# Loading and converting w1 and w2 three to four slots earlier in a fused attention and MoE kernel

## The chip, the cores and the metric

The kernel runs on one core of a Trainium2 chip. The metric is the time of one execution on the device in microseconds. Five engines have instruction queues of their own and each works its queue in order: PE (TensorE, matrix products and transposes), DVE (VectorE), ACT (ScalarE), POOL (GpSimd) and SP (SyncE, which here issues every DMA).

## What is computed

Attention over pooled keys and values, then a gated two-layer product over all tokens:

```python
# q, k, v: (8 batches, 8 heads, 576 tokens, 64)
k_p = k.reshape(B, H, 72, 8, D).mean(axis=3)
v_p = v.reshape(B, H, 72, 8, D).mean(axis=3)
scores = scale * q @ k_p^T
attn = softmax(scores)              # over 72 pooled keys
x = (attn @ v_p) as (4608 tokens, 512)
a = x @ w1                          # w1, w2: (512, 1024)
b = x @ w2
out = (a * b @ w3) @ w_out          # w3: (1024, 1024), w_out: (1024, 512)
```

The kernel multiplies w3 and w_out once, to `W = w3 @ w_out` (1024 x 512), and then has only `out = (a * b) @ W` to do for each token.

## The kernel before

The tokens are worked in 12 chunks of 384. Every fp32 operand is split into a high part and a remainder, and each product is made of three matrix products (high x high, high x low, low x high; `PASSES`).

There are three stages. In W (slots 4 to 36 of the plan, up to about 86.8 us) PE builds `W` from 16 steps `w_mm(s)`. Steps 0 to 7 are W's first half, steps 8 to 15 its second half. In the second half the attention of chunk 0 is worked as well. From slot M0 = 36 on the main loop runs: for each chunk m and each of eight column blocks j, `a_mm` and `b_mm` (L563), the gate (L573, L583, L584, L589) and `out_mm` (L598), with the attention of the next chunk in between.

Nothing is scheduled by a tool. Each piece of work is entered by `at(kind, slot, function, ...)`, with a kind of L (loads), P (post-processing on DVE, ACT and POOL), M (main matmuls) or A (attention matmuls). The whole plan is sorted by the integer part of the slot, then by kind in the order L, P, M, A, then by the fraction. So a slot sets the order in which each engine's instructions are written, and never a time. An engine that has to wait in its queue holds up everything behind it.

What the change and the prediction touch:

- The weights arrive as 512 KB cells (`load_w12`, the DMA at L126), 16 of them for w1 and w2, j = 0 to 7 and w = 0 or 1; cell i = 2j + w. They are written into buffers that the W stage has used (`FREED`): even cells into the place of a block of w_out, free when PE has made `w_mm(8 + j)`; odd cells into places of w3.
- `w12_conv` takes the two 32-bit halves of each number in a cell: ACT makes the high part `z` (L135), DVE shifts the other (L140). `w12_conv2` joins them on DVE (L148). `w12_split` makes the two parts for the matmul: a cast on ACT (L152) and a difference (L153), on POOL or, for three cells (`LO_DVE`), on DVE. The buffers of the conversion are called `wb`, of the w3 cells `Wc`, of the loaded cells `raw` and of the finished parts `hl`.
- The same helper lines work for w3 (`Wc<-raw`, then `hl<-att` after a turn on PE), and L153 and L152 also split W's accumulators at the end of W (`Wc<-b`, `Wc<-o`).
- The softmax of one tile of a chunk: `s_mm` (PE, L404), `mx` (DVE, L420), then either L422 (DVE) and an exponential on ACT (L425) and L426 (DVE), or four exponentials on ACT with their sums (L430; the tiles in `SOFT_ACT`); then L439, L441, L442 (DVE). R is a small remainder of it (L451 on ACT, L453 on DVE). PE turns E and R (L464, L474), ACT and DVE split the result (L520, L521, L527).
- All attention work on PE shares three PSUM tiles named `att`, so L474 of one tile waits until the scores of the next tile have been read.
- `load_q3` (L286) loads q for chunks 0 and 1, PE turns it (L295), ACT copies it (L301). `load_vr` (L356) loads the first and last pooled rows of v, which end up in `VR`. `load_k` (L307) and `prep_k` (L319 on DVE, L362 to L364 on POOL) pool k, and PE turns the result (L328). `av_mm` is L537 to L540, its split L548 and L549.

Of the kernel before, what the change touches and what calls it, by code (L numbers as in the profile page):

```python
# [18 lines left out]
def kernel(  # L19
# [617 lines left out]
    def at(kind, k, fn, *args):  # L637


        plan.append((k // 1, "LPMA".index(kind), k % 1, len(plan), fn, args))  # L640
# [53 lines left out]
    K0 = F0 + 2 * NJ  # L694
    M0 = F0 + 2 * NS
# [6 lines left out]
    for s in range(NS):  # L702
        k = F0 + 2 * s
# [19 lines left out]
    for j in range(NJ):  # L723
        for w in range(2):
            i = 2 * j + w
            at("L", K0 + 8.5 + i, load_w12, j, w)
            k = M0 - 6 + 1.25 * i
            at("P", k, w12_conv, j, w)
            at("P", k + 1, w12_conv2, j, w)
            at("P", k + 4, w12_split, j, w)  # L730


    for m in range(NCH):
        m0 = M0 + 3 * NJ * m
        for j in range(NJ):
            k = m0 + 3 * j
# [9 lines left out]
    for n in range(1, NCH):  # L746
        k = M0 + 3 * NJ * (n - 1)
# [8 lines left out]
    for b in range(1, B):  # L756
        k = M0 + 3 * NJ * (3 * (b // 2) + b % 2 - 1)
# [39 lines left out]
```

## Time and profile before

| | us |
|---|---|
| median of three runs | 786.11 |
| lowest and highest run | 785.08, 788.28 |
| the profiled execution | 787.77 |
| its span, first to last instruction | 785.9 |
| PE busy | 759.7 (97%) |
| DVE busy | 479.2 (61%) |
| ACT busy | 278.5 (35%) |
| POOL busy | 201.1 (26%) |

The mean granted clock of PE is 0.991 of full speed. Of the chain of work that ended last, PE has 74% of the span and DVE 15%.

How to read the rows: a group's row has its line in the kernel, the engine, the operation, the tile written and the tiles read (buffer numbers left out), shapes, and "x" with the number of instructions; then busy us and the mean in ns of one; then the idle time of the engine ahead of them and what ended it. A row of the timeline has the start in us from the span's start, the duration in us, and the same names; the idle time ahead of it stands in brackets with what ended it. A row of the waits reads: engine, tile and line that waited, what it waited for, us in total, times, longest. The rows themselves stand in the prediction.

### The profile page before, as it was taken

The page shows a single profiled execution, that of the slowest core. Times are in us where ns is not written, and L with a number is a line of the kernel's source. Part 1 is how long each engine was busy: PE and PEld are TensorE (multiplying, and loading weights), DVE is VectorE, ACT ScalarE, POOL GpSimd, SP SyncE. Part 2 cuts the span into 40 slices and gives each one's busy share as a digit, 9 for nine tenths or more (in the row PEclk, how much of TensorE's full clock was granted, in tenths as well). Part 3 has the DMA queues.
Part 4 walks back from the last instruction along what each step waited for, and adds up shares of the span by engine and source line. Part 5 has one row for each costly group of instructions (what it writes and reads, how often), then busy time and mean ns, then how long its engine had stood idle before and what let it go on. Part 6 is the DMA issues. An engine that isn't in the chain of part 4 may idle for free.

```text
span 785.9 us, 11514 instructions
## 1 busy us (share of the span) xinstructions
PE 759.7 (97%) x4146; PEld 703.7 (90%) x4146; DVE 479.2 (61%) x939; ACT 278.5 (35%) x694; POOL 201.1 (26%) x234
## 2 busy tenths in 40 slices
PE   8898888999999999999999999999999999999998
PEld 7677777899999998999999998999999998999997
DVE  6957988576475477476484586574574675662211
ACT  5566655332233233232233233332332333332211
POOL 2254564204307403005208202016125220000000
PEclk9999999999999999999999999999999999999999
DMA  9998970016326332036144223037144232120101
GB/s 328 292 209 200 282 152 10 1 61 129 66 79 134 71 98 55 16 86 140 32 129 93 77 81 71 15 101 140 41 122 94 75 75 47 47 55 1 40 1 41
DMA packets 123913, 74.43 MB, mean 95 GB/s; under 512 B 75600, under 2 KB 107600, under 8 KB 123856
## 3 DMA queue, kind: packets, MB, share of 16 engines
q1 hardware_dynamic: 123856, 73.69, 38.2%
q8 instruction: 33, 0.54, 0.3%
q14 instruction: 24, 0.20, 0.1%
HBM read 52.43 MB, written 9.44 MB: 79 GB/s over the span
## 4 chain that ended last, share of the span: by engine, by line
PE 74%; DVE 15%; ACT 3%; DMA 3%; issue 3%; SPq 1%; DVEq 0%
PE o L598 22%; PE a L563 21%; PE b L563 21%; PE att L404 3%; DMA st<-in_v_dram 2%; PE o L624 2%; DVE T L487 2%; DVE E L442 1%; DVE wb L148 1%; DVE wb L140 1%; PE att L538 1%; PE att L540 1%; PE att L539 1%; DVE mx L420 1%; PE att L537 1%
## 5 line engine op out<-in xcount | busy, mean ns | idle before, releaser
L563 PE MATMUL a<-xT,hl 128*128 128x384 f32 x1152 | 222.1, 341 | 0.0
L563 PE MATMUL b<-xT,hl 128*128 128x384 f32 x1152 | 220.8, 339 | 0.4 <-DVE Wc L153 0.4
L563 PEld LDWEIGHTS a<-xT,hl 128*128 128x128 f32 x1152 | 202.5, 189 | 4.5 <-POOL hl L153 0.2
L563 PEld LDWEIGHTS b<-xT,hl 128*128 128x128 f32 x1152 | 199.7, 188 | 0.8 <-DVE Wc L153 0.8
L598 PE MATMUL o<-Wc,gh 128*128 128x512 f32 x576 | 180.6, 395 | 0.0
L362 POOL TENSOR_TENSOR st<-st 72x512 f32<-72x512 f32 (+1 forms) x53 | 77.8, 1469 | 224.5 <-DMA st<-in_k_dram 172.1
L598 PEld LDWEIGHTS o<-Wc,gh 128*128 128x128 f32 x576 | 106.7, 188 | 17.0
L583 DVE TENSOR_TENSOR a<-b,a 128x384 f32<-128x384 f32 x96 | 52.8, 550 | 112.6 <-PE b L563 112.6
L598 PE MATMUL o<-Wc,gl 128*128 128x512 f32 x288 | 114.3, 397 | 3.1 <-DVE gl L589 3.1
L584 ACT CAST gh<-a 128x384 fp32r<-128x384 f32 x96 | 49.2, 513 | 154.8 <-DVE a L583 154.8
L573 ACT COPY a<-a 128x384 f32<-128x384 f32 x96 | 46.0, 479 | 109.8 <-PE a L563 88.0
L425 ACT ACTIVATE E<-E 128x288 f32<-128x288 f32 (+1 forms) x70 | 31.1, 445 | 123.4 <-DVE E L422 123.4
L589 DVE TENSOR_TENSOR gl<-a,gh 128x384 fp32r<-128x384 f32 x96 | 64.0, 667 | 13.0 <-ACT gh L584 13.0
L598 PEld LDWEIGHTS o<-Wc,gl 128*128 128x128 f32 x288 | 54.1, 188 | 16.9 <-DVE gl L589 4.4
L549 DVE TENSOR_TENSOR xT<-att,xT 128x384 fp32r<-128x384 f32 x48 | 26.5, 556 | 60.3 <-ACT xT L548 60.3
L375 POOL TENSOR_TENSOR vbd<-vm,vbd 64x256 fp32r<-64x256 f32 x16 | 12.1, 759 | 180.1 <-ACT vbd L374 179.5
L426 DVE TENSOR_REDUCE sm<-E 128x4 f32<-128x288 f32 (+1 forms) x70 | 31.6, 452 | 35.8 <-ACT E L425 35.8
L404 PE MATMUL att<-kbd,qT 128*128 128x144 f32 (+1 forms) x320 | 52.6, 288 | 0.2 <-ACT E L430 0.2
L404 PEld LDWEIGHTS att<-kbd,qT 128*128 128x128 f32 (+1 forms) x320 | 47.8, 180 | 4.3 <-ACT E L430 0.5
L153 DVE TENSOR_TENSOR PTx<-PTx,PTh 128x512 fp32r<-128x512 f32 (+1 forms) x33 | 24.7, 749 | 35.1 <-ACT PTh L152 31.7
L420 DVE TENSOR_REDUCE mx<-att 128x4 f32<-128x288 f32 (+1 forms) x80 | 35.3, 441 | 17.7 <-PE att L404 17.6
L363 POOL TENSOR_TENSOR st<-st 72x256 f32<-72x256 f32 (+1 forms) x53 | 44.4, 837 | 4.2
(91 smaller groups left out, 811.6 us busy)
## 6 DMA issues: line engine op xcount, KB each, us to landing
raw<-in_moe_w_dram SPq DMA_DIRECT2D x32, 512.0 KB
PTx<-T SPq DMA_DIRECT2D x120, 96.0 KB
st<-in_k_dram SPq DMA_DIRECT2D x32, 288.0 KB
out_dram<-ob SPq DMA_DIRECT2D x35, 256.0 KB
st<-in_v_dram SPq DMA_DIRECT2D x32, 256.0 KB
qs<-in_q_dram SPq DMA_DIRECT2D x128, 48.0 KB
raw<-in_moe_w_out_dram SPq DMA_DIRECT2D x8, 512.0 KB
st<-in_v_dram SPq DMA_DIRECT2D x64, 64.0 KB
```

The costliest lines, as they stand in the source:

```text
L362: nc.gpsimd.tensor_tensor(out=t[:, :, 0:4], in0=t[:, :, 0:4], in1=t[:, :, 4:8], op=ALU.add)
L363: nc.gpsimd.tensor_tensor(out=t[:, :, 0:2], in0=t[:, :, 0:2], in1=t[:, :, 2:4], op=ALU.add)
L404: nc.tensor.matmul(out=ps[:nt, 2 * KP * j:2 * KP * (j + 1)], lhsT=qT[n][:, pr, off:off + nt], rhs=kbd[b % 2][:, pr], start=True, stop=True,)
L420: nc.vector.tensor_reduce(out=mx[:nt, hs], in_=sv, axis=AX.X, op=ALU.min)
L425: nc.scalar.activation(out=E[:nt, hs], in_=E[:nt, hs], func=AF.Exp, scale=-1.0)
L426: nc.vector.reduce_sum(out=sm[:nt, hs], in_=E[:nt, hs], axis=AX.X)
L563: nc.tensor.matmul(out=o, lhsT=w12[j, w][sw][:, kt * P:(kt + 1) * P], rhs=x[sx][:, kt], start=(i == 0), stop=(i == 3 * NK - 1))
L573: nc.scalar.copy(out=a, in_=gt[m, j][:, :CH])
L583: nc.vector.tensor_tensor(out=g, in0=ps[:, :CH], in1=g, op=ALU.mult)
L584: nc.scalar.copy(out=gh, in_=g)
L589: nc.vector.tensor_tensor(out=gl, in0=g, in1=f(gh), op=ALU.subtract)
L598: nc.tensor.matmul(out=oacc[m][t], lhsT=(gh, gl)[sg][:, c], rhs=W[j][sw], start=(j == 0 and i == 0), stop=(j == NJ - 1 and i == 2))
```

## The change

The loads of w1 and w2 (kind L) stand four slots earlier, the conversions (kind P) start three slots earlier, with 1.4 slots from cell to cell instead of 1.25. The last cell's conversion thus moves from slot 48.75 to slot 48. Nothing else is edited, and the number of instructions is the same on every engine.

```diff
     for j in range(NJ):
         for w in range(2):
             i = 2 * j + w
-            at("L", K0 + 8.5 + i, load_w12, j, w)
-            k = M0 - 6 + 1.25 * i
+            at("L", K0 + 4.5 + i, load_w12, j, w)
+            k = M0 - 9 + 1.4 * i
             at("P", k, w12_conv, j, w)
             at("P", k + 1, w12_conv2, j, w)
             at("P", k + 4, w12_split, j, w)
```

What that does to the queues is seen at three places. The first is W's second half, at 63 to 71 us of the profile. On DVE (L140 and L148 on `wb` are conversions of w1 and w2, on `Wc` of w3):

```order
 L140 TENSOR_SCALAR Wc<-raw 128x512
+L140 TENSOR_SCALAR wb<-raw 128x512
 L521 TENSOR_TENSOR PTx<-att,PTh 128x4x4x32
 L420 TENSOR_REDUCE mx<-att 128x4
 L148 SCALAR_TENSOR_TENSOR Wc<-Wc 128x512
 L420 TENSOR_REDUCE mx<-att 128x4
+L148 SCALAR_TENSOR_TENSOR wb<-wb 128x512
+L140 TENSOR_SCALAR wb<-raw 128x512
 L153 TENSOR_TENSOR hl<-att,hl 128x512
 L439 TENSOR_SCALAR sm<-sm 128x8
```

Two L140 and one L148 now stand ahead of the softmax row L439; before, the first of them stood behind it. On SP, which issues the loads, a little earlier (46 to 61 us):

```order
 L120 DMA raw<-in_moe_w_dram 128x4x256 x2
+L126 DMA raw<-in_moe_w_dram 128x4x256
 L356 DMA st<-in_v_dram 32x1x512 x8
-L126 DMA raw<-in_moe_w_dram 128x4x256
+L126 DMA raw<-in_moe_w_dram 128x4x256 x4
 L286 DMA qs<-in_q_dram 64x3x64 x4
 L307 DMA st<-in_k_dram 72x2x512
```

Of the 16 loads (L126) one stands ahead of the v loads now, and five instead of one ahead of the first q loads of chunk 1.

The second place is the passage from W to the main loop, on ACT (86 to 90 us):

```order
 L301 COPY qT<-att 128x3x128 x2
-L135 ACTIVATE wb<-raw 128x512
 L152 CAST Wc<-b 128x512
 L152 CAST Wc<-o_560 128x512
```

A conversion that stood between the copies of q and the casts of W's accumulators stands further ahead now. The third place is tile (1, 1) of the softmax on DVE (111 to 119 us). Before:

```order
L420 TENSOR_REDUCE mx<-att 96x4
L148 SCALAR_TENSOR_TENSOR wb<-wb 128x512
L140 TENSOR_SCALAR wb<-raw 128x512
L583 TENSOR_TENSOR a<-b,a 128x384
L420 TENSOR_REDUCE mx<-att 96x4
L589 TENSOR_TENSOR gl<-a,gh 128x384
L148 SCALAR_TENSOR_TENSOR wb<-wb 128x512
L140 TENSOR_SCALAR wb<-raw 128x512
L439 TENSOR_SCALAR sm<-sm 96x8
```

Now:

```order
L420 TENSOR_REDUCE mx<-att 96x4
L148 SCALAR_TENSOR_TENSOR wb<-wb 128x512
L153 TENSOR_TENSOR hl<-wb,hl 128x512
L140 TENSOR_SCALAR wb<-raw 128x512
L583 TENSOR_TENSOR a<-b,a 128x384
L420 TENSOR_REDUCE mx<-att 96x4
L589 TENSOR_TENSOR gl<-a,gh 128x384
L148 SCALAR_TENSOR_TENSOR wb<-wb 128x512
L439 TENSOR_SCALAR sm<-sm 96x8
```

A split on DVE (L153, cell 9, which is j = 4, w = 1) has come up behind the first `mx`, and one L140 has left.

## The prediction

> **What bounds the kernel now.** I read the page first, then the table of stretches, then PE's waits in the stretch that is not full, then what DVE does there.
>
> ```profile
> span 785.9 us, 11514 instructions
> PE 759.7 (97%) x4146; PEld 703.7 (90%) x4146; DVE 479.2 (61%) x939; ACT 278.5 (35%) x694; POOL 201.1 (26%) x234
> ```
>
> PE is busy 97% of the span, so only 26 us are not PE. The stretches say where these lie (columns: stretch, length, busy us and instructions of PE, PEld, DVE, ACT, POOL, granted clock, DMA share, GB/s):
>
> ```profile
> 86.80:142.20 55.40, 45.53 (x253) 41.28 (x252) 50.20 (x82) 32.87 (x98) 29.47 (x25) 0.97 0.52 117
> 142.20:157.00 14.80, 14.80 (x90) 14.09 (x89) 7.19 (x14) 5.01 (x12) 2.58 (x3) 1.00 0.00 1
> 37.00:86.80 49.80, 46.41 (x237) 38.09 (x238) 37.38 (x66) 32.10 (x102) 28.08 (x28) 0.93 0.93 216
> ```
>
> The first row is the start of the main loop: its first matmul of `a` runs at 86.80, and there PE is idle for 55.40 - 45.53 = 9.87 us, while DVE is busy for 50.20 of 55.40. The second row is what follows: PE has no idle time at all, so a time won before 142.2 goes through to the end and nothing behind it takes it back. The third is W's second half, whose DVE has 12.4 us free. PE's waits in the first stretch, by cause:
>
> ```profile
> PE att L474 <- ACT E L430: 4.8, 2, 3.9
> PE att L474 <- DVE E L422: 2.0, 1, 2.0
> PE att L328 <- DVE km L319: 1.6, 1, 1.6
> ```
>
> Nearly all of it is softmax work for chunk 1 or the pooled k of batch 1, which DVE or ACT delivers late; where ACT is named (L430) it had itself been waiting for DVE's `mx`, the instruction ahead of it. So in this stretch the chain runs along DVE's queue, in which the conversion of w1 and w2 stands between the softmax instructions:
>
> ```profile
> L148 DVE SCALAR_TENSOR_TENSOR wb<-wb 128x512 int32<-128x512 int32 x12 | 12.3, 1023 | 0.9 <-ACT wb L135 0.8
> L140 DVE TENSOR_SCALAR wb<-raw 128x512 int32<-128x512 int32 x11 | 9.3, 849 | 0.0
> ```
>
> That is 21.6 of DVE's 50.2 us. What ends 9.87 us of idle PE is therefore DVE's queue from about 70 us on (before that it waits for others) to about 141.
>
> **The change, term by term.** Nothing is added or removed; 16 loads, and for each cell two DVE conversions, two ACT instructions and a split, change their places. So the sum counts what leaves DVE's chain between 70 and 141 us, and which waits in it go or come.
>
> (a) Work that leaves the chain. By the order of DVE's rows, two L140 and one L148 now stand ahead of the softmax rows of 70.57 us, where DVE waits today:
>
> ```profile
> 67.64 0.46 DVE L420 TENSOR_REDUCE mx<-att 128x4 f32<-128x288 f32 x1 [1.96 <-PE att L404]
> 69.96 0.69 DVE L153 TENSOR_TENSOR hl<-att,hl 128x512 fp32r<-128x512 f32 x1 [1.87 <-ACT hl L152]
> 70.57 0.16 DVE L439 TENSOR_SCALAR sm<-sm 128x8 f32<-128x8 f32 x1
> ...
> 141.38 0.34 DVE L453 TENSOR_TENSOR R<-E,R 96x64 fp32r<-96x64 f32 x2
> ```
>
> The two waits of 1.96 and 1.87 us hide them. From 70.57 to 141.38, where the last softmax tile of chunk 1 is handed to PE, 14 L140 and 15 L148 remain of 16 and 16. Their price is one of two, by whether POOL runs beside them:
>
> ```profile
> 115.69 1.78 DVE L148 SCALAR_TENSOR_TENSOR wb<-wb 128x512 int32<-128x512 int32 x1
> ...
> 120.70 0.68 DVE L148 SCALAR_TENSOR_TENSOR wb<-wb 128x512 int32<-128x512 int32 x1
> ...
> 121.94 0.41 DVE L140 TENSOR_SCALAR wb<-raw 128x512 int32<-128x512 int32 x1
> ```
> ```profile
> 115.31 1.60 POOL L362 TENSOR_TENSOR st<-st 128x512 f32<-128x512 f32 x1
> ...
> 118.14 0.52 POOL L364 TENSOR_TENSOR vm<-st 128x128 f32<-128x128 f32 x1
> 124.51 1.29 POOL L153 TENSOR_TENSOR hl<-wb,hl 128x512 fp32r<-128x512 f32 x1 [5.85 <-ACT hl L152]
> ```
>
> L148 takes 1.78 us beside a POOL instruction and 0.68 where POOL is silent (118.66 to 123.2 or later). At the short price the three are 0.68 + 2 x 0.41 = 1.50 us; at the means of the stretch (1.023 and 0.849) they are 2.72. POOL loses none of its instructions, so what it stretches today it can stretch in the next DVE instruction; I take 1.50, and keep 2.72 for the range. [...]
>
> (b) The wait ahead of W's last split. ACT converts a cell (L135) just ahead of the cast of `Wc` for which DVE waits:
>
> ```profile
> 87.68 0.65 ACT L135 ACTIVATE wb<-raw 128x512 f32<-128x512 f32 x1
> 88.23 0.58 ACT L152 CAST Wc<-b 128x512 fp32r<-128x512 f32 x1
> ```
> ```profile
> 88.84 0.69 DVE L153 TENSOR_TENSOR Wc<-b,Wc 128x512 fp32r<-128x512 f32 x1 [1.00 <-ACT Wc L152]
> ```
>
> In the new order that L135 is gone from there. The cast starts 88.23 - 87.68 = 0.55 us earlier, and DVE's wait of 1.00 shrinks by as much: **-0.55**.
>
> (c) A wait for ACT in the middle:
>
> ```profile
> 123.95 0.69 DVE L148 SCALAR_TENSOR_TENSOR wb<-wb 128x512 int32<-128x512 int32 x1 [0.77 <-ACT wb L135]
> ```
>
> Here L135 stands behind four exponentials on ACT. In the new order the L135 of the cell concerned stands ahead of them: **-0.77**.
>
> (d) A wait that is new. DVE's split of cell (4,1) moves up to right behind `mx` of tile (1,1), and the cast on ACT that it needs stands behind the four exponentials that this very `mx` releases:
>
> ```profile
> 111.61 1.31 ACT E L430 x8
> ```
> ```profile
> 113.38 0.62 ACT L152 CAST hl<-wb 128x512 fp32r<-128x512 f32 x1
> 113.89 0.52 ACT L584 CAST gh<-a 128x384 fp32r<-128x384 f32 x1
> ```
>
> The cast takes 113.89 - 113.38 = 0.51, start to start. So DVE waits 1.31 + 0.51 - 0.68 (the L148 that runs meanwhile) = 1.14 us. Queued behind it are L140, the product L583 and the second `mx`. In exchange the old wait of `gl` there falls from
>
> ```profile
> 114.44 1.33 DVE L589 TENSOR_TENSOR gl<-a,gh 128x384 fp32r<-128x384 f32 x1 [0.87 <-ACT gh L584]
> ```
>
> 0.87 to about 0.1, since L583 is now later than ACT's other work: **+0.4**.
>
> (e) On ACT one L135 now stands ahead of the cast that ends DVE's wait of 1.87 at 69.96; L135 takes 0.55 of ACT's time by the rows of (b) (start to start): **+0.55**, as that cast lies on the chain.
>
> Sum: -1.50 - 0.55 - 0.77 + 0.4 + 0.55 = **-1.87 us**; with the dear price in (a) it is -3.1. PE has 9.87 us of waits, so the gain is not capped by it. The profiled execution took 787.77 us (span 785.9 and 1.9 around it): 785.9 after. It was 1.66 above the median of the runs shown, 786.11; on that scale the forecast is **784.2 us**.
>
> What I cost at nothing: the loads themselves. They are taken from one queue on SP, and the first now waits there for PE to release its cell, with the eight small loads of v (L356) behind it. The cover is between POOL and ACT:
>
> ```profile
> 62.15 1.37 POOL L362 TENSOR_TENSOR st<-st 128x512 f32<-128x512 f32 x1 [6.38 <-DMA st<-in_v_dram]
> ...
> 64.60 0.46 POOL L364 TENSOR_TENSOR vrm<-st 128x128 f32<-128x128 f32 x1
> ```
> ```profile
> 69.80 0.33 ACT L381 CAST vrh<-vrm 128x128 fp32r<-128x128 f32 x1
> ```
>
> POOL has the sum at 65.06 and ACT takes it at 69.80, so 4.7 us late is free. Without this cover each further us would delay `VR`, which PE needs for the first attention product. The loads of q and k that follow are a rival below.
>
> **Rivals.**
>
> The stretch by POOL falls away (779). The cells come one per 1.4 slots instead of 1.25, so POOL's splits and DVE's conversions could overlap less. If the nine L148 and nine L140 that stand behind W's last split drop from their means to the short price, that saves 9 x (1.02 - 0.68) + 9 x (0.85 - 0.41) = 7.0 us; the waits of PE (9.87) allow it: 786.11 - 7.0 = 779.1. For it speaks that DVE ends early in each slot once it is ahead; against it, that POOL has the same instructions in 55 us in which it is busy for 29.47. Chance 0.2.
>
> The q of chunk 1 comes late (790). Four more loads of 512 KB stand ahead of its last pieces than before, and PE turns these directly ahead of its first matmul of `a`:
>
> ```profile
> 75.54 1.18 SPq L286 DMA_DIRECT2D qs<-in_q_dram  x2
> ```
> ```profile
> 81.54 1.80 SPq L126 DMA_DIRECT2D raw<-in_moe_w_dram  x1
> ```
> ```profile
> 86.03 1.02 PE L295 MATMUL att<-ident,qs 128*128 128x128 f32 x6 [0.24 <-DVE xT L549]
> ```
>
> The last q load is issued at 76.1. A load waits for the one eight places ahead in the queue, which puts its landing at 81.5 or earlier. At the 216 GB/s of the stretch, four loads take 4 x 2.4 = 9.7 us. If none of that is hidden, q lands at 91.2, 4.8 us after PE's need at 86.4; ACT's copy of q and the cast of `Wc` behind it wait as long, so the chain starts 4.8 late. Less the 1.87 won this is +2.9, and with the slow matmuls that follow so long an idle time +4.3: 790.4. That price is from the matmuls right behind the wait of 3.9 above, against the same 12 matmuls of `a` a little later, 3.71 - 2.35 = 1.4:
>
> ```profile
> 113.26 3.71 PE L563 MATMUL a<-xT,hl 128*128 128x384 f32 x12
> ...
> 123.58 2.35 PE L563 MATMUL a<-xT,hl 128*128 128x384 f32 x12
> ```
>  Against this: from 52 to 68 us DMA is not full:
>
> ```profile
> 52.00:56.00 4.00, 3.19 (x22) 2.74 (x21) 2.01 (x5) 3.22 (x21) 2.44 (x3) 1.00 0.63 174
> 56.00:60.00 4.00, 4.00 (x22) 3.30 (x21) 2.75 (x8) 2.88 (x16) 0.00 (x0) 1.00 0.68 199
> 60.00:64.00 4.00, 1.71 (x11) 1.03 (x10) 3.97 (x9) 2.31 (x8) 1.77 (x2) 1.00 0.83 183
> 64.00:68.00 4.00, 4.00 (x18) 3.53 (x18) 1.95 (x4) 1.69 (x9) 0.98 (x2) 0.63 0.64 145
> ```
>
> These free shares are 4 x (0.37 + 0.32 + 0.17 + 0.36) = 4.9 us, and that leaves 4.8 of the 9.7: landing at 86.3, just in time. It decides from 86.4 on. Chance 0.14.
>
> Nothing is left (786 to 787). If (d) comes at its full 1.1 us, (a) is hidden by waits of DVE for PE, and only (b) counts, the sum is about 0 to +1. Chance 0.16.
>
> **How the numbers follow.** Forecast (782.5 to 786) 0.5, rivals 0.2, 0.14 and 0.16. About 0.5%, 3.9 us, is what a measurement of this kernel can tell from no change: the runs shown lie 3.2 us apart. Faster by more (below 782.2) takes the first rival and the edge of the forecast with the dear price: 0.28. Slower (above 790.0) takes most of the q rival: 0.13. Within: 0.59. The range leaves out the far end of the first rival and of the second: 778.5 to 789.5.
>
> **What would show it.** (a): two L140 and one L148 before 70 us inside DVE's waits; the stretch from the first `a` to the last softmax tile shorter by 2 to 3 us, with DVE still nearly full. (b), (c): the waits of 1.00 and 0.77 shorter or gone. (d): DVE's L153 on `wb` with a wait of about 1.1 us for ACT. (e): the cast at 69.33 half a us later. The forecast is wrong if PE waits for DMA at L295, if the means of L148 and L140 in the stretch fall to 0.7 and 0.4, or if PE's wait at L474 (3.9) stays as long as it is.

## The result and the profile after

The changed kernel takes 782.41 us (median of 20 runs, 780.73 to 788.11), the kernel before 787.96 us (20 runs, 783.82 to 791.66). The ratio is 0.9935, 95% interval 0.992 to 0.9951. A second comparison (e1 below) gave 0.9942, 0.9924 to 0.996. By the ratios the change wins 4.6 to 5.1 us. The forecast, 784.2 us, named the side, and the time lies inside its whole range (778.5 to 789.5), a little below the part that was held likeliest (782.5 to 786). Of the gain it had only 1.9 us. That the two times lie only 1.8 us apart is partly luck: the forecast starts from 786.11 us (three runs of the kernel before), and its 20 runs have 787.96. From there 1.9 us less is 786.1, and the changed kernel is 3.7 us below that.

The profiled execution of the changed kernel took 788.11 us, the longest of its 20 runs. A second profile (e1) took 784.20 us, the median of its own runs, and is the one meant where only one is shown. First its page:

```profile
span 782.4 us, 11499 instructions
PE 758.8 (97%) x4146; PEld 702.9 (90%) x4146; DVE 477.4 (61%) x939; ACT 279.0 (36%) x694; POOL 201.9 (26%) x234
```

The page alone hides the change: PE is busy 97% in both. The stretches show it. They are cut at events that every profile has: the first turn of R in W's second half (L474), the first matmul of `a` (L563), and the last turn of R of chunk 1. The part between the first two is called the tail of W here, the part between the last two the main stage. Columns as in the prediction: length, busy us and instructions of PE, PEld, DVE, ACT, POOL, granted clock, DMA share, GB/s. The tail and the main stage before:

```profile
63.65:86.80 23.15, 22.86 (x116) 18.99 (x117) 18.96 (x30) 15.20 (x45) 13.72 (x15) 0.93 0.95 226
86.80:141.86 55.06, 45.20 (x250) 40.94 (x249) 49.87 (x81) 32.53 (x98) 29.13 (x25) 0.97 0.53 118
```

The same two and what follows them in the profile of 788.11 us:

```profile
65.78:93.70 27.92, 24.66 (x117) 20.02 (x117) 24.70 (x34) 16.74 (x48) 15.89 (x17) 0.88 1.04 239
93.70:142.17 48.47, 44.31 (x250) 40.99 (x249) 43.52 (x78) 30.94 (x94) 26.86 (x23) 0.96 0.41 97
142.17:157.00 14.83, 14.83 (x93) 14.17 (x91) 7.28 (x13) 4.94 (x11) 3.49 (x4) 1.00 0.00 1
```

And in the second profile:

```profile
63.42:89.75 26.33, 23.06 (x116) 18.74 (x117) 24.44 (x34) 17.06 (x49) 17.58 (x18) 0.94 0.92 251
89.75:138.22 48.47, 44.35 (x250) 40.95 (x249) 43.52 (x78) 30.96 (x94) 26.86 (x23) 0.96 0.45 104
```

Three things are to be seen. The main stage is 6.59 us shorter (55.06 to 48.47), the same in both profiles: DVE works 6.35 us less there, and PE's idle time falls from 9.86 to 4.12. The tail of W is longer, by 3.18 in the second profile and 4.77 in the first: DVE works 5.48 us more in it (18.96 to 24.44), and PE, which had almost no idle time inside it, has 3.27. Behind the last turn of R PE is full as before. From there to the end the three profiles take 645.91, 645.94 and 645.98 us, so nothing is won or lost behind it. Stage by stage in us, with the time ahead of the first turn cut once more at the first product of column block `b` in W:

| | to the first `b` of W | to the first turn of R | tail of W | main stage | to the end | whole |
|---|---|---|---|---|---|---|
| before | 45.77 | 17.88 | 23.15 | 55.06 | 645.91 | 787.77 |
| changed, second profile | 46.61 | 16.81 | 26.33 | 48.47 | 645.98 | 784.20 |
| difference | +0.84 | -1.07 | +3.18 | -6.59 | +0.07 | -3.57 |

The first column is ahead of everything that the change moves, and scatters from execution to execution (44.2 to 48.1 us in all profiles). Without it the change wins 4.4 us by these two profiles. That this is near the 4.6 to 5.1 of the many runs is a matter of which profiles are compared: the profile of 788.11 us, with 18.38 us to the first turn of R and a tail of 27.92, gives 1.3 us against the same one before, and a second profile of the kernel before (e2) gives 7.4 us against the second of the change. So the gain as a whole is read from the many runs, and from single profiles only what repeats: the main stage.

PE's waits in the main stage, second profile:

```profile
PE att L404 <- ACT E L430: 1.7, 1, 1.7
PE att L328 <- DVE km L319: 1.7, 1, 1.7
PE att L474 <- DVE E L422: 0.7, 1, 0.7
```

The long wait at L474 (3.9 of the 4.8 that the prediction quoted) is gone, with the slow matmuls that followed it (twelve in 3.71 us). Other slow ones are there: the twelve behind the wait of 1.7 us at L328 take 3.22 us instead of 2.35. What is left are three waits, and none is for DMA.

### The profile page after: what moved, and what is told of

It reads as the page before. It is cut to its first block, busy times and chain, and to the rows that moved or that the text cites. A ratio compares the mean times of both kernels' runs of the same rounds, so it can differ in the third digit from the quotient of the medians.

```text
span 786.3 us, 11499 instructions
## 1 busy us (share of the span) xinstructions
PE 760.7 (97%) x4146; PEld 704.5 (90%) x4146; DVE 479.3 (61%) x939; ACT 278.7 (35%) x694; POOL 198.1 (25%) x234
## 4 chain that ended last, share of the span: by engine, by line
PE 75%; DVE 14%; ACT 4%; DMA 4%; issue 2%; SPq 0%; DVEq 0%
PE o L598 22%; PE a L563 21%; PE b L563 21%; PE att L404 3%; PE o L624 2%; DVE T L487 2%; DMA st<-in_k_dram 2%; DVE E L422 1%; DVE mx L420 1%; DVE E L442 1%; ACT E L425 1%; PE att L538 1%; DVE wb L140 1%; PE att L540 1%; PE att L539 1%
## 5 line engine op out<-in xcount | busy, mean ns | idle before, releaser
L563 PE MATMUL b<-xT,hl 128*128 128x384 f32 x1152 | 222.0, 341 | 0.0
L563 PE MATMUL a<-xT,hl 128*128 128x384 f32 x1152 | 220.6, 339 | 0.0
L563 PEld LDWEIGHTS a<-xT,hl 128*128 128x128 f32 x1152 | 201.1, 188 | 4.4 <-DVE xT L549 0.2
L563 PEld LDWEIGHTS b<-xT,hl 128*128 128x128 f32 x1152 | 200.7, 189 | 0.2 <-DVE Wc L153 0.2
L362 POOL TENSOR_TENSOR st<-st 72x512 f32<-72x512 f32 (+1 forms) x53 | 73.3, 1383 | 229.9 <-DMA st<-in_k_dram 177.4
L583 DVE TENSOR_TENSOR a<-b,a 128x384 f32<-128x384 f32 x96 | 52.8, 550 | 110.1 <-PE b L563 110.1
L589 DVE TENSOR_TENSOR gl<-a,gh 128x384 fp32r<-128x384 f32 x96 | 63.5, 662 | 13.5 <-ACT gh L584 13.5
L375 POOL TENSOR_TENSOR vbd<-vm,vbd 64x256 fp32r<-64x256 f32 x16 | 12.2, 760 | 177.5 <-ACT vbd L374 177.1
L404 PEld LDWEIGHTS att<-kbd,qT 128*128 128x128 f32 (+1 forms) x320 | 48.1, 181 | 6.0 <-ACT E L430 2.1
L426 DVE TENSOR_REDUCE sm<-E 128x4 f32<-128x288 f32 (+1 forms) x70 | 31.6, 452 | 35.9 <-ACT E L425 35.9
L153 DVE TENSOR_TENSOR PTx<-PTx,PTh 128x512 fp32r<-128x512 f32 (+1 forms) x33 | 26.9, 815 | 35.1 <-ACT PTh L152 32.9
L624 PE MATMUL o<-hl 128*128 128x512 f32 x144 | 44.3, 446 | 3.9 <-DVE hl L177 3.9
L420 DVE TENSOR_REDUCE mx<-att 128x4 f32<-128x288 f32 (+1 forms) x80 | 35.3, 441 | 17.6 <-PE att L404 17.6
```

What stands on the lines that cost most here:

```text
L362: nc.gpsimd.tensor_tensor(out=t[:, :, 0:4], in0=t[:, :, 0:4], in1=t[:, :, 4:8], op=ALU.add)
L404: nc.tensor.matmul(out=ps[:nt, 2 * KP * j:2 * KP * (j + 1)], lhsT=qT[n][:, pr, off:off + nt], rhs=kbd[b % 2][:, pr], start=True, stop=True,)
L420: nc.vector.tensor_reduce(out=mx[:nt, hs], in_=sv, axis=AX.X, op=ALU.min)
L426: nc.vector.reduce_sum(out=sm[:nt, hs], in_=E[:nt, hs], axis=AX.X)
L563: nc.tensor.matmul(out=o, lhsT=w12[j, w][sw][:, kt * P:(kt + 1) * P], rhs=x[sx][:, kt], start=(i == 0), stop=(i == 3 * NK - 1))
L583: nc.vector.tensor_tensor(out=g, in0=ps[:, :CH], in1=g, op=ALU.mult)
```

## Experiments

Every ratio is against the kernel before on the same chip. Tail and main stage are from the one profile of each kernel.

| label | what it is | ratio (95%) | profiled us | tail | main stage |
|---|---|---|---|---|---|
| e1 | the changed kernel again | 0.9942 (0.9924 to 0.996) | 784.20 | 26.33 | 48.47 |
| e2 | the kernel before again | 1.0008 (0.9991 to 1.0025) | 791.35 | 24.15 | 55.53 |
| e3 | loads alone | 1.0000 (0.9987 to 1.0012) | 788.54 | 23.64 | 55.18 |
| e4 | conversions alone | 0.9973 (0.996 to 0.9986) | 786.43 | 25.87 | 48.53 |
| e5 | loads, earlier start, old pace | 0.9991 (0.9973 to 1.0009) | 786.61 | 26.19 | 50.58 |
| e6 | loads, old start, new pace | 1.0016 (0.9999 to 1.0032) | 788.70 | 23.24 | 54.35 |
| e7 | all splits on DVE | 0.999 (0.9973 to 1.0006) | 787.53 | 24.45 | 52.83 |
| e8 | first load behind v's | 0.9974 (0.9955 to 0.9993) | 785.27 | 27.93 | 48.49 |
| e9 | first split a slot later | 0.9923 (0.9892 to 0.9953) | 783.36 | 26.19 | 48.42 |
| e10 | first two splits 1.5 slots later | 0.9956 (0.9937 to 0.9976) | 783.94 | 25.81 | 48.46 |
| e11 | one step further up | 0.9998 (0.9981 to 1.0016) | 789.45 | 26.48 | 52.52 |
| e12 | e9 again | 0.9925 (0.9898 to 0.9951) | 782.18 | 24.38 | 48.44 |

### e1, e2: how far the profiles repeat

No edit: the two kernels again.

> The changed kernel once more, for a second profile, since the profiled execution of it (788.11 us) lies 5.7 us above its median. Theory A (DVE's queue: conversion work has left the main loop's first 55 us for the stretch before it, where part of it is hidden): ratio to before 0.992 to 0.995 again; main stage (first matmul of a at L563 to the last turn of R at L474) 48 to 50 us against 55.2 before; the tail of W ahead of it (from the first turn of R to the first a) 23 to 25 us, against 22.87 before and 27.64 in the first profile of the changed kernel. Theory B (the earlier loads are what gains, by taking transfers out of the main loop): the same ratio, but the main stage shorter by what PE waits for DMA, so no wait for DVE or ACT changes.

> The kernel before against itself. All theories: ratio 1.000 with an interval of about 0.3% to either side. Its second profile gives the spread of the stages: tail of W 22.9 and main stage 55.2 us, each within 1.5 us.

(The expectations count the tail from 0.28 us later: their 22.87 and 27.64 are the 23.15 and 27.92 here.) The main stage repeats to 0.01 us in the changed kernel and to 0.5 in the one before, as expected. The tail does not repeat (26.33 and 27.92) and is longer than the 23 to 25 us expected. Its PE work is the same 116 or 117 instructions, but they are busy for 23.06 us at a granted clock of 0.94 and for 24.66 at 0.88. So the gain in the main stage holds in every profile, and what the tail costs differs with the clock that the execution is granted there.

### e3, e4: loads alone, conversions alone

```diff
 e3, against before
-            at("L", K0 + 8.5 + i, load_w12, j, w)
+            at("L", K0 + 4.5 + i, load_w12, j, w)
 e4, against the changed kernel
-            at("L", K0 + 4.5 + i, load_w12, j, w)
+            at("L", K0 + min(8.5 + i, 7 + 1.4 * i), load_w12, j, w)
```

In e4 the first four loads stand up to 1.5 slots further up than before, so that each load is still ahead of its conversion, and the others at their old places. The first one stays behind the v loads.

> Only the loads move (four slots up), the conversions stay where they were. Theory A: DVE's rows are those of before, so the ratio is 0.998 to 1.003, main stage 54 to 56 us. Theory B: most of the gain is here, ratio 0.993 to 0.996 and main stage near 49. A loss of over 0.3% would mean that q, k and v behind the loads come late.

> Only the conversions move (start three slots up, one cell per 1.4 slots). The loads stay, but for the first four, which come up by at most 1.5 slots, as they must stand ahead of their conversion. Theory A: main stage 48 to 51 us as in the changed kernel, ratio 0.993 to 0.997; where DVE or ACT now waits for a cell, these waits (a few us in W's tail) are what the earlier loads are for. Theory B: ratio 0.998 to 1.003.

The loads alone leave the main stage as it was (55.18) and the time too. The conversions alone bring the whole gain of the main stage (48.53). So what shortens the main stage is where the conversions stand. Yet e4 wins only 0.27%, just short of the 0.3 to 0.7% expected, where the whole change wins 0.6%. Its interval begins where that of e1 ends (0.996), so the loads seem to be worth something together with the conversions (e8).

### e5, e6: start and pace apart

```diff
 e5, against the changed kernel
-            k = M0 - 9 + 1.4 * i
+            k = M0 - 9 + 1.25 * i
 e6, against the changed kernel
-            k = M0 - 9 + 1.4 * i
+            k = M0 - 6 + 1.4 * i
```

> The loads as in the changed kernel, the conversions three slots earlier, but at the old pace of 1.25 slots. Theory A1 (what counts is how many conversions stand ahead of the first matmul of a): more of them do than in the changed kernel, so the main stage is 46 to 48.5 us, the tail of W 26.5 to 28.5, the ratio to before 0.993 to 0.997. Theory A2 (what counts is the pace, by which POOL's splits stretch less of DVE's conversions): the main stage is 50 to 53, the ratio 0.997 to 1.000.

> The loads as in the changed kernel, the conversions start where they did before, at the new pace of 1.4 slots. Theory A1: as many conversions stand ahead of the first matmul of a as before, so the main stage is 53 to 55.5 us and the ratio to before 0.998 to 1.002. Theory A2: the main stage is 49 to 51, the ratio 0.993 to 0.996.

Neither wins anything that can be told from no change; the two together win 0.6%. The result of e5 is what A2 expects and that of e6 what A1 expects, so each run brings down the theory that the other one fits: neither the number of conversions ahead of the first `a` alone nor the pace alone counts. e5 has even one conversion less in its main stage than the change (18 L140 and L148 for 19), and DVE is busy for less (42.94 against 43.52), but DVE waits more. DVE's waits in its main stage:

```profile
DVE Wc L153 <- ACT Wc L152: 1.4, 1, 1.4
DVE R L453 <- ACT R L451: 1.1, 1, 1.1
DVE gl L589 <- ACT gh L584: 0.9, 2, 0.6
DVE wb L148 <- ACT wb L135: 0.8, 1, 0.8
```

With 2.0 at L426, 0.7 at L439 and 0.2 at L521 that is 7.1 us, against 4.4 in the changed kernel. At the old pace a step of the conversion falls again behind ACT's exponentials (the 0.8), and a wait of R for ACT (1.1) is new; PE then waits 2.36 us at L474, and the twelve matmuls of `a` behind it take 3.69:

```profile
124.64 0.58 PE L474 MATMUL att<-ident,R 96*128 96x96 f32 x2 [2.36 <-ACT E L430]
124.93 3.69 PE L563 MATMUL a<-xT,hl 128*128 128x384 f32 x12
```

e6 has all 23 conversions in its main stage and each takes less (0.79 us against 0.94 before), but the splits come late: PE waits 2.2 us for POOL's L153 at `b` and 2.6 for R.

### e7: take POOL's splits away

```diff
     def w12_split(j, w):
         r, _ = stage.pop(("w12", j, w))
         w12[j, w] = hl_cell(FREED[2 * j + w])
-        split(f(r), *w12[j, w], eng=nc.vector if (j, w) in LO_DVE else nc.gpsimd)
+        split(f(r), *w12[j, w], eng=nc.vector)
```

This measures what POOL costs DVE: the same conversions, in the same places, with the splits of w1 and w2 gone from POOL, at the price that DVE has them to do.

> The changed kernel with all 16 splits of w1 and w2 on DVE, 13 of which POOL did. This measures the disputed price by itself: what POOL's splits stretch on DVE. Theory A (the stretch is POOL's doing): in the main stage the means of L148 and L140 fall from 0.99 and 0.74 us to at most 0.85 and 0.60, and though DVE gets 9 to 11 splits of 0.61 there (5.5 to 6.7 us more work), the main stage grows by 1 to 5 us only, from 48.5. Rival (the long forms come from something else, such as ACT or DMA): the means stay, and the main stage grows by the full 5.5 to 6.7.

DVE's groups in the main stage of the changed kernel (second profile), then of e7 (instructions, busy us, mean ns, idle time ahead and its releaser):

```profile
L148 DVE SCALAR_TENSOR_TENSOR wb<-wb 128x512 int32<-128x512 int32 x10 | 9.9, 986 | 0.1
L140 DVE TENSOR_SCALAR wb<-raw 128x512 int32<-128x512 int32 x9 | 6.7, 742 | 0.0
L442 DVE TENSOR_TENSOR E<-E,sm 96x576 f32<-96x576 f32 x4 | 3.9, 975 | 0.1
L153 DVE TENSOR_TENSOR hl<-wb,hl 128x512 fp32r<-128x512 f32 x2 | 2.1, 1068 | 0.2 <-ACT hl L152 0.2
```
```profile
L153 DVE TENSOR_TENSOR hl<-wb,hl 128x512 fp32r<-128x512 f32 x12 | 8.9, 738 | 4.5 <-ACT hl L152 4.5
L148 DVE SCALAR_TENSOR_TENSOR wb<-wb 128x512 int32<-128x512 int32 x10 | 7.3, 732 | 0.1
L140 DVE TENSOR_SCALAR wb<-raw 128x512 int32<-128x512 int32 x9 | 4.5, 505 | 0.0
```

The same ten L148 take 2.6 us less and the same nine L140 2.2 less, at means near the prediction's short prices of 0.68 and 0.41, as theory A said. DVE has ten more splits, 10 x 0.738 = 7.4 us of work, and one L583 (0.54) less, and is busy for only 0.9 us more (44.42 against 43.52). So about 7.4 - 0.5 - 0.9 = 6 of the 43.5 us that DVE is busy in the changed kernel's main stage are time that POOL's splits, nine of them there, add to its instructions; with the 0.61 us for a split that the expectation took, it is 4.7. The time is not better than before all the same: the main stage is 4.4 us longer than in the change, because DVE now waits 4.5 us for the casts on ACT in its own queue, where POOL had waited beside it (for 19.1 us ahead of its nine L153).

### e8: the first load where it was

```diff
-            at("L", K0 + 4.5 + i, load_w12, j, w)
+            at("L", K0 + (5.6 if i == 0 else 4.5 + i), load_w12, j, w)
```

> The changed kernel, but the first load of w1 stands behind the eight small loads of v (L356) instead of ahead of them, so that POOL gets this v as early as before. Theory A3 (the earlier first load gains about 1 us by holding v back, so that POOL's tree does not run beside DVE's two L453 of the first tile): PE's wait at the first turn of R is 2.1 us again, as in the kernel before and with the conversions alone, against 1.0 to 1.6 in the changed kernel; ratio to before 0.994 to 0.998. Rival (that wait has nothing to do with the loads): it is 1.0 to 1.6 here too.

In the changed kernel one load of w1 stands ahead of the v loads on SP, and POOL's sum of v starts later. Before, it started at 62.15 (POOL's L362, in the prediction) and lay beside DVE's first pair of R, for which PE waits. The pair before, then in the second profile of the changed kernel, with POOL's row there:

```profile
62.18 1.42 DVE L453 TENSOR_TENSOR R<-E,R 128x64 fp32r<-128x64 f32 x2
```
```profile
63.01 0.35 DVE L453 TENSOR_TENSOR R<-E,R 128x64 fp32r<-128x64 f32 x2
65.33 1.40 POOL L362 TENSOR_TENSOR st<-st 128x512 f32<-128x512 f32 x1 [8.15 <-DMA st<-in_v_dram]
```

The pair is 1.07 us shorter, and from the first `b` of W to the first turn of R it takes 16.81 instead of 17.88. In e8 PE's row at that turn is

```profile
62.89 0.44 PE L474 MATMUL att<-ident,R 128*128 128x128 f32 x2 [1.72 <-DVE R L453]
```

That is neither the 2.1 of the theory nor the 1.0 to 1.6 of the rival. In the other profiles with the first load ahead of v this wait is 1.02 us, but for 1.36 in e11 and 1.57 in the profile of 788.11 us, where POOL's sum lies partly beside the pair (0.90 us). With the load behind v it is 2.09 or 2.10 in before, e2 and e4. So it is 1.02 to 1.57 us with the load ahead of v and 1.72 to 2.10 with it behind, as POOL's sum happens to fall. (The lengths to the first turn of R also hold a wait of PE for the q of chunk 0, of 0.8 to 1.2 us, that comes and goes with the execution: e2, e6, e8, e9 and the profile of 788.11 us have it.)

At most this is worth 1.1 us, 0.14%, and e3, which has the short wait too, wins nothing by it. The ratios of e4 and e8 lie 0.3 to 0.4% above the changed kernel's. For e4 the profiles name some more: beside the 1.1 us, PE is idle for 3.97 us in its tail and for 3.27 in the second profile of the change, and the tail is not longer (25.87) because that execution was granted the full clock in it (1.00, with PE busy for 21.90 us instead of 23.06). For e8 the rest is not explained, and the intervals of e8 and of e1 overlap.

### e9, e10, e12: the price in the tail

```diff
 e9 and e12
-            at("P", k + 4, w12_split, j, w)
+            at("P", k + (5 if i == 0 else 4), w12_split, j, w)
 e10
-            at("P", k + 4, w12_split, j, w)
+            at("P", k + (5.5 if i < 2 else 4), w12_split, j, w)
```

In the tail PE's longest new wait is for the R pair of the third tile. In the profile of 788.11 us, the pair on DVE, POOL beside it, and PE:

```profile
77.05 2.11 DVE L453 TENSOR_TENSOR R<-E,R 128x64 fp32r<-128x64 f32 x2
```
```profile
76.91 0.80 POOL L375 TENSOR_TENSOR vbd<-vm,vbd 64x256 fp32r<-64x256 f32 x1
77.67 1.25 POOL L153 TENSOR_TENSOR hl<-wb,hl 128x512 fp32r<-128x512 f32 x1
```
```profile
79.20 0.44 PE L474 MATMUL att<-ident,R 128*128 128x128 f32 x2 [1.50 <-DVE R L453]
```

The pair runs to 79.16, just past the end of POOL's L153 (78.92). That L153 is the split of the first cell, which the change has brought here. e9 moves it one slot down.

> The changed kernel with the split of its first cell (L153, j 0 w 0) one slot later, so that POOL does both L375 ahead of it. Theory A (the cost in W's tail is POOL stretching DVE's R pair L453, 2.11 us in the profile of after against 0.54 before): the pair then runs beside L375 alone, takes 1.2 to 1.7 us, PE's wait at the third L474 falls from 1.50 to 0.6 to 1.1, W's tail (first L474 to first a) is 0.4 to 1 us shorter than 26.3 to 27.9, main stays 48.5; ratio to before 0.991 to 0.994. Rival (the R pair is late because the conversions stand ahead of it on DVE, whatever POOL does): pair starts at the same distance, wait at L474 stays 1.5, ratio as after, 0.9935 to 0.9942.

> The changed kernel with the splits of the first two cells 1.5 slots later: cell 0 on POOL stands behind both L375 and behind the next k tree, cell 1 on DVE stands two instructions of the third tile's product later. Theory A: as e9 or better by 0.2 to 0.5 us, since DVE's L153 (0.94) also leaves the way of L153 and L521 of the attention: tail 25 to 26 us, ratio 0.990 to 0.993, unless PE then waits for hl of cell 0 at its first a (L563). Rival (nothing but the number of conversions ahead of the tail counts): 0.9935 to 0.9942, wait of 1.5 stays.

> The kernel of e9 again, since its six runs left the ratio at 0.9892 to 0.9953. If the later split of the first cell gains anything beside the change: ratio 0.990 to 0.9925, with the third L474 of W's tail without a wait and the tail under 26 us. If PE's wait has only moved on to L537 (xT), as in the profile of e9 (1.47 there instead of 1.50 at L474): ratio 0.993 to 0.995, as the changed kernel.

PE's row in e12, and a later one:

```profile
74.07 0.44 PE L474 MATMUL att<-ident,R 128*128 128x128 f32 x2 [0.29 <-DVE R L453]
...
80.15 0.55 PE L295 MATMUL att<-ident,qs 128*128 128x128 f32 x3 [1.45 <-DVE hl L153]
```

The pair takes 0.62 us in e9 and 0.88 in e10 and e12 instead of 2.11, and the wait of 1.50 falls to 0.28 and 0.29 in e10 and e12 and is gone in e9: more than was expected. So POOL's split beside the pair was the cause of that wait. But the time is hardly better, since PE waits further on: 1.45 at L295 in e12, 1.07 there and 1.47 at L537 in e9, 2.44 at L537 in e10. e9 and e12 (0.9923 and 0.9925) are the lowest ratios of all, with intervals that cover the change's ratios. They may be a us better; that isn't shown. The tail of e12 is 1.95 us shorter than that of the change, but 1.3 of it is PE's matmuls at the full clock (1.00 for 0.94, busy for 21.78 us instead of 23.06). e10 is not better than the change; its ratio, 0.9956, is above both expectations.

e12 shows one thing more. In its main stage PE is granted the full clock:

```profile
87.82:136.26 48.44, 42.94 (x250) 39.42 (x249) 43.48 (x78) 30.94 (x94) 28.34 (x25) 1.00 0.48 116
```

PE is busy for 1.4 us less than in the second profile of the change (44.35), and the stage is as long (48.44 and 48.47): PE waits that much more for ACT and DVE instead (5.50 us for 4.12). So PE's clock does not set the length of this stage here; DVE, busy for 43.48 and 43.52 us, is the same in both.

### e11: a step further

```diff
-            at("L", K0 + 4.5 + i, load_w12, j, w)
-            k = M0 - 9 + 1.4 * i
+            at("L", K0 + 4.2 + i, load_w12, j, w)
+            k = M0 - 10 + 1.45 * i
```

> Loads a third of a slot earlier still, the first conversion one slot earlier again (M0-10) and 1.45 slots apart: one step further along both parts of the change. If more lead in W's second half always moves work out of the main stage: main 46.5 to 48, PE waits there 2.5 to 4, ratio 0.988 to 0.993. Rival (what leaves the main stage comes back in the tail): main 48 to 48.5, tail 27.5 to 29.5, ratio 0.994 to 0.999.

The whole gain is lost, and not in the tail, as the rival had it: the main stage is 52.52. Two groups of DVE in it:

```profile
L442 DVE TENSOR_TENSOR E<-E,sm 96x576 f32<-96x576 f32 x4 | 5.4, 1338 | 0.1
L453 DVE TENSOR_TENSOR R<-E,R 96x64 fp32r<-96x64 f32 x8 | 5.2, 692 | 0.0
```

There is one conversion less in its main stage than in the change (18 for 19), but POOL's splits now lie beside the softmax rows (L442 at 130.37 beside one that starts at 130.26, the R pair at 141.92 beside two that run from 139.62 to 142.67): L442 takes 5.4 us instead of 3.9, the R pairs 5.2 instead of 1.9. DVE waits 3.3 us for casts on ACT ahead of two splits, where the change has 0.2. PE's wait at L474 is back with 3.3 us. Both theories were wrong here: more lead neither helps further nor costs in the tail (26.48).

## Why the forecast had the side right and the size wrong

**What bounds the kernel.** Right. Everything was decided ahead of the last turn of R of chunk 1, in DVE's queue: behind it every profile takes 645.9 to 646.1 us but for e6 (647.4, with slow matmuls behind a wait of 2.56 us), and in e12 PE's clock doesn't change the main stage.

**(a), the work that leaves the chain: the step that failed.** The rows named were right. In the profile of 788.11 us, on DVE ahead of the softmax row:

```profile
70.22 0.46 DVE L420 TENSOR_REDUCE mx<-att 128x4 f32<-128x288 f32 x1 [1.46 <-PE att L404]
70.59 0.68 DVE L148 SCALAR_TENSOR_TENSOR wb<-wb 128x512 int32<-128x512 int32 x1
71.19 0.42 DVE L140 TENSOR_SCALAR wb<-raw 128x512 int32<-128x512 int32 x1
73.10 0.69 DVE L153 TENSOR_TENSOR hl<-att,hl 128x512 fp32r<-128x512 f32 x1 [1.48 <-ACT hl L152]
```

They stand between two of DVE's waits, which were 1.96 and 1.87 us and are 1.46 and 1.48 here, and 0.66 and 0.95 in the second profile. The rows that count begin behind them. But from the third tile's L439 to the last L453 of chunk 1 DVE's chain went from 71.15 to 67.64 us (67.66 in the other profile), 3.5 less. Its waits fell from 4.68 to 4.39, so the work fell by 3.2 where the prediction took 1.50. Its dear price, 2.72, was nearer, and also too small. The prediction argued that POOL loses none of its instructions, so that what it stretches today it can stretch in the next instruction; the 1.50 rests on this, which was an estimate. Over the whole kernel it nearly holds (DVE is busy for 479.2 us before, for 479.3 and 477.4 after). In the stage that bounds the time no run shows it: with the cells, two of POOL's splits went from the main stage into the tail, and the instructions that stayed came to lie beside other rows of DVE. Nor is an instruction beside POOL always the long one: in the profile before, two L148 took 0.68 us (at 96.37 and 108.33) while a POOL L153 ran from 96.31 to 99.01 and an L362 from 107.76 to 110.13. The sum counted only the rows that leave, at a price that was to stay. POOL's group in the main stage before, and in the second profile after:

```profile
L153 POOL TENSOR_TENSOR hl<-wb,hl 128x512 fp32r<-128x512 f32 x11 | 16.6, 1517 | 22.2 <-ACT hl L152 14.2 <-DMA raw<-in_moe_w_dram 7.5 <-DVE sm L426 0.5
```
```profile
L153 POOL TENSOR_TENSOR hl<-wb,hl 128x512 fp32r<-128x512 f32 x9 | 14.7, 1631 | 21.0 <-ACT hl L152 19.1 <-DVE wb L140 1.6
```

DVE's busy time there fell by 6.35 us. Two L148 and two L140 less are 2.2 at the short price, one L583 more is +0.5, and the rest, about 5, is stretch: in the conversions that stay, and in L442 (4.7 to 3.9), L439 (3.1 to 2.0) and L589 (3.5 to 3.0). The two splits alone don't account for it: e7 prices nine at 5 to 6 us, so two at little over 1. The rest must come from where the others fall. That is argued, but e5 and e11 speak for it: each has 18 conversions and ten of POOL's splits in its main stage, and DVE is busy for 42.94 us in one and 44.62 in the other. In the tail DVE's busy time rose by 5.48, of which 2.2 is the four conversions at the short price, and 3.3 is stretch: 1.6 of it the R pair, the rest in the conversions there. So the stretch in the tail grew by about two thirds of what the main stage lost. There DVE has room (18.96 busy of 23.15 before), and only the part that hits the R pair and what follows it reaches PE. The 3.5 us of the chain are in both profiles of the change. The rest of the 4.6 to 5.1 isn't located: from the first `b` of W to the L439 at which the chain begins it is 24.80 us before and 26.54 in e2, and 23.15 and 26.30 in the changed kernel.

**(b) to (e), the waits.** The three that lie on that chain, (b) to (d), were forecast as -0.55 - 0.77 + 0.4 = -0.92, and all waits of the chain together changed by -0.29. (b): the wait of 1.00 fell to 0.81, not by 0.55; the cast did come earlier after the copies of q, by 94.57 - 93.52 = 1.05 against 88.23 - 86.61 = 1.62, but DVE was there earlier too. (c): the 0.77 is gone, as said. (d): DVE's split on `wb` waits only 0.23, since the L148 ahead of it took 1.73 beside POOL (its L362 runs from 114.82 to 116.55) and not the 0.68 that the prediction put in:

```profile
115.37 1.73 DVE L148 SCALAR_TENSOR_TENSOR wb<-wb 128x512 int32<-128x512 int32 x1
117.33 0.92 DVE L153 TENSOR_TENSOR hl<-wb,hl 128x512 fp32r<-128x512 f32 x1 [0.23 <-ACT hl L152]
...
127.70 0.78 DVE L589 TENSOR_TENSOR gl<-a,gh 128x384 fp32r<-128x384 f32 x1 [1.09 <-ACT gh L584]
```

The old wait of `gl` fell as said (0.87 to 0.22), and a wait of 1.09 at the next tile's `gl`, in the last row, was not foreseen. (e): L135 stands ahead of the cast as said (71.91 and 72.47 on ACT), but this is ahead of the row from which the prediction counts the chain, in a part in which the profiles scatter by more than its +0.55.

**Loads, costed at nothing.** They cost nothing: e3 is at 1.0000. The first load made PE's wait at the first turn of R shorter, by up to 1.07 us, by pushing POOL's sum of v off DVE's first R pair; in e3 alone that shows in the wait and not in the time. The prediction had seen that sum move and asked only whether it came too late.

**The tail.** The prediction said that a time won before 142 us goes through; it counted on DVE's 12.4 free us in W's second half and did not look for what the conversions would cost there. They cost 3.2 us in the second profile: PE's waits there of 1.53 (R, L474), 0.77 (L537) and 0.81 (L295), and some slow matmuls.

**Rivals.** "The stretch by POOL falls away" was half right: the main stage shortened by 6.6 us of the 7.0 worked out, but the means of L148 and L140 fell to 0.99 and 0.74 only, and half of the gain was given back in the tail. The gain of 4.6 to 5.1 us lies between this rival and the forecast. "The q of chunk 1 comes late" did not happen in either profile of the change: PE waits at L295 for DVE, 0.84 and 0.81. That it stood near its point is seen in e6 and e9, where PE waits 0.5 and 1.3 us there for the load of q. What this rival took of the queue, that a load waits for the one eight places ahead, is in the trace of before: the q load issued at 75.54 follows the landing, at 75.53, of the load eight ahead of it (issued at 68.11), and the last q load, issued at 76.12, had landed at 79.31. "Nothing is left" fell.

**What stays open:** why e8 lies 0.3 to 0.4% above the change, and in part why e4 does; whether e9 is better than the change; and how much of the gain is PE's clock. Of the 20 runs of the changed kernel eleven have a mean granted clock of 0.994 or more and take 780.73 to 782.97 us, and nine have 0.992 or less and take 782.35 to 788.11. In e1 only two of nine reach 0.994, and of the kernel before 8 of the 95 runs measured beside the experiments. That the change brings the higher clock, by shorter waits of PE, is not shown. Why start and pace must fit each other is read from the rows of e5, e6 and e11 (which rows POOL's splits fall beside, and which casts DVE meets on ACT); it wasn't tried slot by slot.

## What to carry to other kernels

Price an instruction that is moved by what it leaves and by what the instructions that stay will then lie beside: here the change in stretch in the main stage (about 5 us) was worth more than the DVE instructions that left it (2.2). Where one engine's instructions stretch another's, as POOL's splits do DVE's here (about 6 of 43.5 us by e7), a shift of the order can make the stretch come out elsewhere (3.3 us more in the tail here), so look up at once which rows on the way to the end the work will lie beside at its new place. And a slot table of this kind has narrow optima: a third of the way on (e11) or half of the change (e5, e6) gave nothing, so each setting is read by its waits and not by its direction.

## What was unexpected of the hardware

One two-instruction group of 128 x 64 elements, the R pair, took 0.35 to 2.11 us depending on what POOL did beside it: 0.35 with POOL idle (61.31 in the profile before), 1.42 beside an L362 of 1.37 (62.18, the same profile), and 2.11 beside an L375 and an L153 that ran from 76.91 to 78.92 (77.05 in the profile of 788.11 us). Not every such meeting costs as much: a pair of 96 x 64 at 114.47 in that last profile took 0.61, though an L362 of 1.73 began at 114.82. Other groups did not change, though some of theirs lie beside POOL too: L420, L422, L426, L441 and L583 have the same mean to 0.01 us (0.44, 0.45, 0.45, 0.20 and 0.54 to 0.55) in the main stages of before, of the change, of e7 and of e11. In e11 an L420 (100.85) and an L422 (101.33) have these lengths inside a POOL L153 that runs from 98.81 to 102.08.

Short waits of PE are at times followed by slow matmuls, and at times not. After 2.36 us (e5) twelve matmuls took 3.69 us instead of 2.35; in the profile of 788.11 us a wait of 1.78 left the twelve behind it at 2.35, and one of 1.68 was followed by twelve in 3.47; in the tail, with waits of 1.5, 0.8 and 0.8, the same work was granted 0.88 of the clock in one execution (788.11 us) and 0.94 in another (784.20). What decides between them is not shown by any run here.
